# Two small DMAs ahead of ScalarE's first work: one word of every eighth row of x[0] and of w_in

## The chip, the cores and the metric

The kernel runs on one core of a Trainium2 chip. The metric is the device time of one execution in microseconds (us); the median over several executions is compared. A core has five engines that run beside each other, each with its own queue of instructions: PE (TensorE, the matmuls; PEld is its weight load), DVE (VectorE), ACT (ScalarE), POOL (GpSimd) and SP (SyncE, which here only issues DMAs). ScalarE, GpSimd and SyncE issue DMAs from their own instruction queues; sixteen DMA engines move the data for all of them.

## The reference, cut to what matters

```
x:     8 x 8 x 512 x 64   (batch, head, token, dim)
state: 8 x 8 x  32 x 64
attention, per batch and head:
  xread = softmax(x @ state.T / 8) @ state      # 512 x 64
  sread = softmax(state @ x.T / 8) @ x          #  32 x 64
  rows  = concat(xread, sread), heads side by side   # 544 rows of 512 per batch
MoE-like layer on the 8 * 544 = 4352 rows:
  h   = rows @ w_in                  # w_in 512 x 2048
  g   = h + sin(alpha * h)**2 / (alpha + 1e-9)
  out = g @ w_out                    # w_out 2048 x 512, out 4352 x 512 fp32
```

All inputs are fp32 in HBM; the matmuls run in bf16.

## The kernel before

The work is cut into named steps, the methods of the class Steps. The string ORDER lists them, with their arguments, in the order in which they are given out; every engine gets its own instructions in that order, and waits between engines are put in from the data. There is nothing else that schedules: moving a step in ORDER moves its instructions on each engine that it uses.

The steps that matter at the start are these.

- Loads. `l_alpha` (line 222) puts alpha's 16 rows of 128 words into SBUF, issued by ScalarE. `l_s01` (L229) loads the states of batches 0 and 1, and `lq` (L241) loads x of batch 0 in four parts of two heads each, both issued by SP in fp32. All other loads are issued by GpSimd and cast to bf16 on the way: `li` (L262) a quarter of w_in's columns, `lx` (L255) x of a later batch, `l_st` (L247) the other states, `lo` (L268) a quarter of w_out.
- `exp_table` and `sin_table` are one-element activations that bring in ScalarE's tables for Exp and Sin (each shows as an ACT_TABLE_LOAD and an ACTIVATE, L217 and L220).
- `warm_up` (L277) issues matmuls on zeros.
- `al_t` transposes alpha on TensorE (L294); `al_c` and `inva` make alpha and 1/alpha on VectorE. `s01_c`, `s01_t`, `s01_k` bring the first states into their transposed form stT.
- `xq` (L330, ScalarE) casts a part of x[0] to bf16, `xtq` transposes it, `xc` (L362) copies it out as xT. `sc`, `ex`, `rs`, `rr`, `nm` are scores, exponential, row sums, reciprocal and the normalised A. `at` and `ac` transpose A of batch 0 on TensorE; for later batches `ad` (L420, SP) does it as a DMA transpose into AT.
- The first matmul of the layer takes two halves: `m` (L468) multiplies state and w_in into M, copied out by `me` (L476), and `h` or `hg` (L493, L508) multiplies M and AT. `si`, `sq`, `gt` make g, and `o` (L543) multiplies g and w_out; `oc` and `os` copy and store the result.

ORDER begins, before the change:

```
l_alpha l_s01 consts lq.0.S zero.0 ident_ exp_table warm_up.6.512.0 zero.1 lq.1.S lq.2.S identf.V
lq.3.S s01_c.G li.0 xq.0.A al_t.1 s01_t.2 lx.1.0.1 al_c xq.1.A inva xtq.0.3 s01_k.1.V s01_k.0.A li.1
```

So ScalarE's queue starts with the issue of alpha's load, the Exp table load and the dummy Exp, and then waits for the first part of x. TensorE starts with six warm-up matmuls, and then has alpha's transpose.

Of the kernel before, what the change touches and what calls it, by code (L numbers as in the profile page):

```python
# [13 lines left out]
FP32 = mybir.dt.float32  # L14
# [4 lines left out]


ORDER = """
l_alpha l_s01 consts lq.0.S zero.0 ident_ exp_table warm_up.6.512.0 zero.1 lq.1.S lq.2.S identf.V
lq.3.S s01_c.G li.0 xq.0.A al_t.1 s01_t.2 lx.1.0.1 al_c xq.1.A inva xtq.0.3 s01_k.1.V s01_k.0.A li.1
xtq.1 xq.2.A xc.0.0.0.V warm_up.2.128.4 warm_up.2.128.5 xc.0.0.1.V l_st xq.3.A xtq.2.6 sc.0.0.7
xc.0.1.0.V lo.0 xtq.3 ex.0.0 xc.0.1.1.V warm_up.2.128.0 warm_up.2.128.1 warm_up.2.128.2
# [126 lines left out]
class Steps:  # L152
# [65 lines left out]

    def sin_table(k):
        k.nc.scalar.activation(k.tiny[:, 1:2], k.warm[:, 0:1], ACT.Sin)  # L220

    def l_alpha(k):
        k.alpha_rows = k.const.tile([k.FT, k.P], FP32, name="alpha_rows")
        k.nc.scalar.dma_start(k.alpha_rows[:], k.alpha.rearrange("(ft p) -> ft p", p=k.P))
# [395 lines left out]
```

## Time and profile before

| | |
|---|---|
| median of 4 runs | 225.77 us (225.35, 225.46, 226.09, 227.63) |
| the profiled execution | 227.63 us, of which the span in the profile is 225.8 us |
| PE busy | 212.5 us, 94% of the span |
| ACT, DVE, POOL busy | 172.3, 167.9, 109.0 us |
| bytes read from HBM and written to it | 17.44 and 8.91 MB |
| granted TensorE clock, mean | 0.992 of full speed |

The profile shows one execution. Its page gives the busy time of each engine, the span in 40 slices of 5.6 us with the busy share of each as a digit (9 is 90% or more), the TensorE clock that was granted in each slice, and the share of the time in which the 16 DMA engines were moving packets. The chain is the work that ended last, followed back from the last instruction to what released it. In a timeline a line gives start, duration, engine, line, operation and operands, and in brackets how long the engine was idle before it and what ended the wait. An engine name with a q (ACTq, SPq) is an instruction that issues a DMA. "To landing" is the time from a DMA's issue to its completion.

### The profile page before, as it was taken

To read this page: it belongs to the slowest core of one execution; us is meant where nothing else is said; L and a number is where in the kernel's file an instruction comes from. 1 tells how busy PE (TensorE), PEld (TensorE's weight loads), DVE (VectorE), ACT (ScalarE), POOL (GpSimd) and SP (SyncE) were. 2 spreads that over 40 slices of the span, in tenths; PEclk is the share of its full clock that TensorE was granted. 3 is DMA by queue.
4 is the path that set the end of the run, shared out by engine and by line. 5 is a ranking of instruction groups with operands and counts; after the bars stand their busy time and mean duration, and the time that the engine had idled before them with its cause. 6 is when DMAs were issued, how large, how long until landed. Compare 5 with 4: busy or idle time off the path is not lost.

```text
span 225.8 us, 4227 instructions
## 1 busy us (share of the span) xinstructions
PE 212.5 (94%) x1575; PEld 102.4 (45%) x1575; DVE 167.9 (74%) x292; ACT 172.3 (76%) x291; POOL 109.0 (48%) x117
## 2 busy tenths in 40 slices
PE   6678994999999999999999999999999999999993
PEld 2444441343544344444443444444446465555641
DVE  4768773599999989887999877798874779875210
ACT  4789894599999999895997698799861599794111
POOL 6759550385817585786372544196022057451000
PEclk9999998899999999999999999999999999999999
DMA  6999993096795221567514536460026111101332
GB/s 208 174 207 206 208 197 39 15 160 202 138 186 105 85 46 52 107 124 160 75 46 84 152 96 104 77 191 4 0 93 94 50 49 46 46 0 49 90 97 93
DMA packets 37828, 23.48 MB, mean 104 GB/s; under 512 B 20768, under 2 KB 33456, under 8 KB 37808
## 3 DMA queue, kind: packets, MB, share of 16 engines
q1 hardware_dynamic: 26128, 15.08, 24.9%
q0 software_dynamic: 11648, 8.13, 24.8%
q8 instruction: 12, 0.20, 0.4%
q14 instruction: 8, 0.07, 0.1%
q10 hardware_dynamic: 32, 0.01, 0.0%
HBM read 17.44 MB, written 8.91 MB: 117 GB/s over the span
## 4 chain that ended last, share of the span: by engine, by line
PE 84%; ACT 5%; DMA 4%; DVE 4%; issue 1%; POOL 0%
PE o_ps L543 50%; PE h_ps L493 22%; DMA AT<-A 4%; PE m_ps L468 3%; PE h_ps L499 3%; PE w_ps L430 2%; ACT s L516 2%; PE warm_ps L277 2%; PE s_ps L378 1%; DVE gT L532 1%; PE w_ps L441 1%; ACT M L476 1%; ACT L220 1%; DVE R L389 1%; POOL A L195 0%
## 5 line engine op out<-in xcount | busy, mean ns | idle before, releaser
L543 PE MATMUL o_ps<-w_out_sb,gT 128*128 128x512 bf16 (+1 forms) x560 | 137.2, 376 | 0.5 <-DVE stT L314 0.5
L195 POOL TENSOR_TENSOR s<-s 128x512 bf16<-128x512 bf16 (+1 forms) x80 | 80.6, 1020 | 70.7 <-ACT s L516 62.7
L532 DVE SCALAR_TENSOR_TENSOR gT<-s,inva_sb,h_ps 128x512 bf16<-128x512 bf16 (+1 forms) x144 | 97.0, 713 | 18.3 <-POOL s L195 11.9
L516 ACT ACTIVATE s<-h_ps,alpha_sb 128x512 bf16<-128x512 f32 (+1 forms) x144 | 88.6, 669 | 11.5 <-PE h_ps L493 8.8
L543 PEld LDWEIGHTS <-gT 128*128 128x128 bf16 x560 | 53.1, 98 | 60.6 <-issue 5.7
L493 PE MATMUL h_ps<-AT,M 128*128 128x512 bf16 x224 | 61.5, 381 | 3.1 <-DMA AT<-A 3.1
L493 PEld LDWEIGHTS <-M 128*128 128x128 bf16 x224 | 21.6, 98 | 28.4 <-DMA AT<-A 3.6
L525 ACT ACTIVATE s<-s 128x512 bf16<-128x512 bf16 (+1 forms) x54 | 32.3, 605 | 0.9
L476 ACT CAST M<-m_ps 128x512 bf16<-128x512 f32 x36 | 19.5, 592 | 9.9 <-PE m_ps L468 9.8
L551 ACT COPY o_sb<-o_ps 128x512 f32<-128x512 f32 (+1 forms) x14 | 7.8, 557 | 22.3 <-PE o_ps L543 22.2
L195 POOL TENSOR_TENSOR A<-E,rR 128x512 bf16<-128x512 bf16 x14 | 14.5, 1049 | 18.9 <-issue 7.2
L476 DVE CAST M<-m_ps 128x512 bf16<-128x512 f32 x28 | 18.4, 677 | 4.3 <-PE m_ps L468 4.1
L551 DVE COPY o_sb<-o_ps 128x512 f32<-128x512 f32 x21 | 14.3, 687 | 9.3 <-PE o_ps L543 9.0
L389 DVE TENSOR_REDUCE R<-E 128x16 f32<-128x512 bf16 x16 | 10.4, 666 | 0.7 <-ACT E L385 0.6
L468 PE MATMUL m_ps<-w_in_sb,stT 64*32 64x512 bf16 x256 | 10.6, 382 | 0.3 <-ACT xT L362 0.2
L508 PE MATMUL h_ps<-AT,M 128*128 128x512 bf16 x32 | 9.1, 381 | 1.7 <-ACT M L476 1.5
L448 DVE RECIPROCAL rC<-w_ps 128x128 f32<-128x128 f32 x8 | 7.5, 942 | 4.2 <-PE w_ps L441 4.2
L385 ACT ACTIVATE E<-s_ps 128x512 bf16<-128x512 f32 x16 | 8.9, 596 | 1.4 <-PE s_ps L378 1.3
L499 PE MATMUL h_ps<-xs_all,w_in_sb 128*128 128x256 bf16 x64 | 8.9, 273 | 0.0
L516 ACT ACT_TABLE_LOAD x6 | 7.7, 1283 | 0.9 <-PE h_ps L493 0.8
L322 DVE COPY xp<-xnat 128x1024 bf16<-128x1024 bf16 x14 | 7.1, 534 | 1.0 <-DMA xnat<-in_x_dram 1.0
L385 ACT ACT_TABLE_LOAD x6 | 7.7, 1283 | 0.1
(57 smaller groups left out, 96.1 us busy)
## 6 DMA issues: line engine op xcount, KB each, us to landing
out_dram<-o_sb SPq DMA_DIRECT2D x33, 256.0 KB, 2.4
xnat<-in_x_dram POOLq DMA_DIRECT2D x7, 512.0 KB, 6.3
w_in_sb<-in_moe_w_in_dram POOLq DMA_DIRECT2D x4, 512.0 KB, 13.1
w_out_sb<-in_moe_w_out_dram POOLq DMA_DIRECT2D x4, 512.0 KB, 18.0
x<-in_x_dram SPq DMA_DIRECT2D x4, 256.0 KB, 3.7
st_nat<-in_state_dram POOLq DMA_DIRECT2D x1, 256.0 KB, 12.2
out_dram<-o_sb SPq DMA_DIRECT2D x2, 128.0 KB, 2.7
s<-in_state_dram SPq DMA_DIRECT2D x1, 128.0 KB, 2.1
```

Of the source, the lines that this page charges most:

```text
L195: {"V": k.nc.vector, "G": k.nc.gpsimd}[eng].tensor_tensor(out, a, b, ALU.mult)
L385: k.nc.scalar.activation(E[:, g], k.t["sc", b, g][:], ACT.Exp, scale=k.scale)
L389: k.nc.vector.reduce_sum(R[:, g], k.t["E", b][:, g].rearrange("p c (h j) -> p (c h) j", j=k.Ns), axis=AX.X)
L468: k.nc.tensor.matmul(k.t["m", b, s + n, g][o0:o0 + k.Ns, :], k.stT[k.half(r), b * k.G + g, c0:c0 + k.Ns], k.w_in_sb[k.half(r), 2 * g + h, ...
L476: k.copy(eng)(k.t["M", b][:, g, s * k.FW:(s + 1) * k.FW], k.t["m", b, s, g][:])
L493: k.nc.tensor.matmul(hp[:, :n], k.t["M", t][:, g, fs], k.t["AT", t][:, g, :], start=(g == 0), stop=(g == k.G - 1),)
L499: k.nc.tensor.matmul(hp[:, :n], k.w_in_sb[:, q, fs], k.xs_all[:, q].rearrange("p b j -> p (b j)"), start=(q == 0), stop=(q == k.Q - 1),)
L516: k.nc.scalar.activation(s[:, :n], k.t["h", t, f][:, :n], ACT.Sin, scale=k.alpha_sb[:, f:f + 1])
L525: k.nc.scalar.activation(s2[:, :n], s[:, :n], ACT.Square)
L532: k.nc.vector.scalar_tensor_tensor(gT[:, :n], k.t["s2", t, f][:, :n], k.inva_sb[:, f:f + 1], k.t["h", t, f][:, :n], ALU.mult, ALU.add,)
L543: k.nc.tensor.matmul(k.t["o", t, st, half][:, cols], k.t["gT", t, f][:, rows], k.w_out_sb[:, f, cols], start=(f == 0), stop=(f == k.FT - 1),)
L551: k.copy(eng)(o_sb[:, cols], k.t["o", t, st, half][:, cols])
```

## The change

Two new steps, `touch_x` and `touch`, stand first in ORDER, ahead of `l_alpha`. Each issues one DMA from ScalarE's queue into a tile of its own which nothing reads. `touch_x` takes the first word of every eighth 1 KB row of each head of x[0]: 16 rows for each of 8 heads. `touch` takes the first word of every eighth row of w_in: 16 rows in each of the four groups of 128 rows. Every word is a run of 4 bytes by itself.

```diff
 ORDER = """
-l_alpha l_s01 consts lq.0.S zero.0 ident_ exp_table warm_up.6.512.0 zero.1 lq.1.S lq.2.S identf.V
+touch_x touch l_alpha l_s01 consts lq.0.S zero.0 ident_ exp_table warm_up.6.512.0 zero.1 lq.1.S lq.2.S identf.V
...
+    def touch(k):
+        k.touched = k.const.tile([16, k.Q], FP32, name="touched")
+        k.nc.scalar.dma_start(
+            k.touched[:].unsqueeze(2), k.w_in.rearrange("(q p) f -> p q f", p=k.P)[::8, :, 0:1]
+        )
+
+    def touch_x(k):
+        k.touched_x = k.const.tile([16, k.H], FP32, name="touched_x")
+        k.nc.scalar.dma_start(
+            k.touched_x[:].unsqueeze(2),
+            k.x[0].rearrange("h (p i) d -> p h (i d)", i=k.C)[::8, :, 0:1],
+        )
```

## The prediction

> **What bounds the kernel now.** I read first the page's busy rows with the slices, then the chain that ended last in its first 40 us, then the timeline of the start and of the place where TensorE falls idle, then short windows, and last the DMA transfers.
>
> ```profile
> PE   6678994999999999999999999999999999999993
> PEclk9999998899999999999999999999999999999999
> DMA  6999993096795221567514536460026111101332
> PE 84%; ACT 5%; DMA 4%; DVE 4%; issue 1%; POOL 0%
> ```
>
> Each digit is a slice of 5.6 us. TensorE is full from the eighth slice (39.5 us) to the end, and the chain is TensorE for 84% of the span. Only the first six or seven slices have room, and there the DMA engines are full. An edit that touches only the start can move the end only through the moment at which TensorE becomes full. This is the chain around both edges of that stretch:
>
> ```profile
> 1.19 2.74 PE warm_ps L277 x6
> 3.93 0.23 PE al_ps L294
> ...
> 28.29 9.12 DMA AT<-A
> ```
>
> At its front stand the six warm-up matmuls, then the transpose of alpha, which is next in TensorE's order, and through al_c, inva and s01_k it reaches the scores. At its back stands the DMA transpose of batch 1's A, and there TensorE runs dry (timeline, then windows whose columns are the busy time of PE, PEld, DVE, ACT and POOL, PEclk, the DMA share and GB/s):
>
> ```profile
> 37.45 0.60 PE L493 MATMUL h_ps<-AT,M 128*128 128x512 bf16 x2 [3.15 <-DMA AT<-A]
> 34.70:38.20 3.50, 0.75 (x4) 0.40 (x5) 1.35 (x3) 0.54 (x2) 0.00 (x0) 0.99 0.17 19
> 38.20:41.60 3.40, 3.40 (x10) 0.89 (x9) 0.75 (x1) 1.96 (x3) 0.04 (x1) 0.50 0.01 2
> ```
>
> TensorE waits 3.15 us for AT, and the 3.4 us after it run at half the clock. The transpose is not slow by itself: the seven have a median of 3.1 us from issue to landing, this one 9.1. It shares the engines with the queued loads: the DMA share is 1.23 from 28 to 30 us and 1.35 from 30 to 34, and the last load of that backlog, batch 2's xnat, lands 21.1 us after its issue at 16.14, so at 37.2, just before AT at 37.4. **So the start is bound by the bytes of the load stream, and the work in front of TensorE has 3.15 us to spare.**
>
> **The change, part by part.** It removes nothing. It puts two DMA issues ahead of all that ScalarE does, with 16x8 and 16x4 single words, 192 words of 4 bytes, on a queue of its own that so far carried alpha's rows alone. The instruction orders of the other engines are the same in both programs. The eight DMA semaphores go round in turn, so each SP transfer now uses one two places on, and AT's issue gains a wait for touch_x, which is over some 25 us earlier: nothing.
>
> ```profile
> 0.73 0.42 ACTq L224 DMA_DIRECT2D alpha_rows<-in_moe_alpha_dram  x1
> 1.19 1.28 ACT L217 ACT_TABLE_LOAD   x1 [1.19 <-PEq L604]
> 1.20 1.95 SPq L241 DMA_DIRECT2D x<-in_x_dram  x4
> 2.48 0.20 ACT L217 ACTIVATE tiny<-warm 128x1 f32<-128x1 bf16 x1
> 3.94 0.62 ACT L330 CAST xp<-x 128x512 bf16<-128x512 f32 x1 [1.26 <-DMA x<-in_x_dram]
> ```
>
> (1) *ScalarE's issue time.* An issue takes 0.42 us here for alpha and 1.95/4 = 0.49 on SP, so two cost 0.84 to 0.98; I take 0.9. Behind them wait alpha's issue, the Exp table load (1.28) and the dummy Exp (0.20). These end at 2.68 now and at 3.58 then. ScalarE next waits for x until 3.94 (1.26 us idle), so 0.36 of the cover is left and the price is nothing. Without that cover it is 0.9.
>
> (2) *Alpha's landing.* Issued at 0.73, alpha's last completion is in the trace at 2.60, 1.87 later. Issued at 1.63 it lands at 3.50. TensorE wants it at 3.86, after the warm-ups; 0.36 of cover is left, if the words ahead of it do not hold up its queue.
>
> (3) *The words themselves.* 192 words on 16 engines are 12 on each. No transfer of such words is in the trace. The nearest rows are its packet records: a 1024-byte packet of x takes 0.046 us, a 4-byte completion record 0.009, a first 512-byte packet of alpha up to 0.116. So 12 words are 0.11 to 0.55 us per engine, spent between 1.95 (where alpha's first packet stands now) and 2.85 (where it would then stand): alpha is not delayed by them. [...] I take 0.046, so 0.55 us per engine, and keep a twelve times larger value for the slow rival.
>
> (4) *The loads beside them.* From 2.0 to 3.0 us the DMA share is 0.71 and 0.85, so some 0.2 us per engine is free. The other 0.35 falls on state and x: x lands up to 0.35 later (3.92, 4.84, 5.90, 6.60 now). ScalarE's four casts of x sit on or close to the chain there, so the cost to the start is 0 to 0.35.
>
> (5) *What it may give.* First accesses are visibly slow. Of the 1061 packets of state and x before 5.2 us 19 took over 0.1 us, 3.6 us together, 2.7 above the usual. Of the first w_in packets (5.2 to 7 us) seven took 0.42 to 0.87 instead of 0.098, 3.3 us above it. If the touches take all that on themselves, 6.0/16 = 0.38 us per engine comes off the load stream. The touch of x can save little of its part: it is issued at 0.73, the loads of x themselves from 1.20. I take 0.2 for w_in. An earlier w_in helps no compute: m waits only 0.30 us for it, and then for ScalarE, which is in the Sin table load and the AT copy until 11.56. It helps only if AT lands earlier. But the last backlog load ends on thirteen engines by 35.2 and on the last three at 37.0 to 37.2. One of the late engines was late at w_in's first slice (10.64 against 9.30 for the other fifteen); others fell behind at 16 and 28 us, where the records show an instruction fetch of 16 KB. AT waits for all of them, so the saving at the end is 0 to 0.2. I take 0.
>
> **Sum.** A start 0 to 0.35 us later goes into the 3.15 us for which TensorE waits for AT; A is ready that much later, yet AT still lands with the end of the backlog. Change: 0, with -0.2 and +0.35 (if AT follows its issue after all) as ends. The profiled execution took 227.63 us, 225.80 of it span, and is the slowest of the four; the median is 225.77. That spread is larger than any term above. The half clock after the gap, 3.4/2 = 1.7 us, would explain it if not every execution has it. [...] I leave it out of the sum and put it in the range. **Forecast: 225.7 us, no change.** A measurement of this kernel tells about 1%, 2.3 us, from no change.
>
> **The rivals.**
>
> *Faster.* The touches clear the first accesses on the engine that is last, and AT lands up to 1.34 us earlier (10.64 - 9.30). The gap then is below 2 us and the half clock goes for good: 1.34 + 1.7 = 3.0, so 222.7 us. For it: the slow first packets are real, and there is one late engine from w_in's first slice on. Against it: two other engines are as late by 37 us for another reason.
>
> *Slower.* The touches pay the cold price word by word: 12 words at the mean of the seven cold w_in packets (4.0/7 = 0.57) are 6.8 us on each engine. Alpha then lands near 1.95 + 6.8 + 0.65 = 9.4 instead of 2.60, where 0.65 is what it takes now from first packet to last completion. Alpha's transpose starts 5.5 us later, the idle wait gives back 3.15, and 2.4 us remain; the load stream, which shares these engines, would lose as much again where it cannot pass them. I put it at +3.5, so 229.2 us. It decides against me from alpha landing later than 3.86 + 3.15 = 7.0 us. For it: each touched row of w_in may be a first access. Against it: only some ten of the first packets of w_in were cold, not one for each row.
>
> *It does not do what it says.* The touches run beside the first loads instead of ahead of them, and the same cold packets appear as before. Time: 225.8; this is inside no change.
>
> **How the numbers follow.** Forecast together with the idle touch 0.76, faster 0.11, slower 0.13. The middle case has -0.2 to +0.35 from the terms and about one us on either side from the half clock that comes and goes: 224.6 to 226.9. Cut into both rivals until no more than 2 in 10 is left out: 224.0 to 227.8. The chances of over 1% faster, within 1% and over 1% slower are the three above.
>
> **What would show it.** In the profile after: the Exp table load begins near 2.1 us and the first cast of x still near 3.9 to 4.3; al_ps starts between 3.86 and 4.3; AT lands at 37 to 38 us, and TensorE's wait for it is 2.5 to 3.5 us; few w_in packets over 0.4 us. The forecast is wrong if al_ps starts after 7 us, if AT lands before 36 or after 39 us, or if TensorE has a new idle stretch after 45 us.

## The result, and the profile after

The changed kernel takes 225.62 us (median of 35 runs, 224.73 to 228.53), the kernel before, with its runs on the same chips, 226.46 us (56 runs, 225.07 to 228.96). The ratio is 0.9966, with a 95% interval of 0.9947 to 0.9986: a third of one per cent, or 0.77 us, faster. The ratios, and the counts and means of executions below, leave out runs that took over 1.5% longer than the fastest of their kernel. The profiled execution took 224.96 us, 223.2 of it span, against 225.8 before. That is 2.6 us less, three times what the medians differ by, so the pair of profiles must not be read as the effect.

First the slices and the chain's shares of the page after:

```profile
PE   5868999999999999999999999999999999999993
PEclk9999999999999999999999999999999999999999
DMA  6999995494876302759215438440017111101322
PE 84%; ACT 5%; DMA 4%; DVE 3%; issue 1%; POOL 0%; ACTq 0%
```

The dip that TensorE had in its seventh slice is gone, and the clock row has no 8 any more. The chain in the first 40 us, in order of time, shows what stands at both edges now:

```profile
1.67 3.22 DMA alpha_rows<-in_moe_alpha_dram
...
5.02 0.27 PE al_ps L308
...
30.29 6.35 DMA AT<-A
```

At the front stands alpha's load instead of the warm-ups. Alpha's transpose starts at 5.02 instead of 3.86 us, A is ready and AT issued at 30.29 instead of 28.29, and AT lands at 36.6 instead of 37.4. So in this pair of executions the work in front came 2 us later, and the wait behind it ended 0.8 us earlier. The timeline of the changed kernel's start, and then the first matmul on AT:

```profile
0.73 0.42 ACTq L231 DMA_DIRECT2D touched_x<-in_x_dram  x1
1.19 0.45 ACTq L225 DMA_DIRECT2D touched<-in_moe_w_in_dram  x1
1.67 0.47 ACTq L238 DMA_DIRECT2D alpha_rows<-in_moe_alpha_dram  x1
2.17 1.28 ACT L217 ACT_TABLE_LOAD   x1 [2.17 <-issue]
3.46 0.20 ACT L217 ACTIVATE tiny<-warm 128x1 f32<-128x1 bf16 x1
4.56 1.32 ACT L344 CAST xp<-x 128x512 bf16<-128x512 f32 x2 [0.89 <-DMA x<-in_x_dram]
5.02 0.25 PE L308 MATMUL al_ps<-ident_f,alpha_rows 16*128 16x16 f32 x1 [1.09 <-DMA alpha_rows<-in_moe_alpha_dram]
9.03 1.49 PE L291 MATMUL warm_ps<-warm 128*128 128x128 bf16 x12
36.68 0.60 PE L507 MATMUL h_ps<-AT,M 128*128 128x512 bf16 x2 [0.37 <-DMA AT<-A]
```

The last line is the main one: TensorE waits 0.37 us for AT where it waited 3.15. The twelve warm-ups at 9.03 take 1.49 us; in the timeline before they take 0.83:

```profile
7.87 0.83 PE L277 MATMUL warm_ps<-warm 128*128 128x128 bf16 x12
```

So TensorE ran at 0.56 of that speed there, although the clock row shows a 9: the trace's clock record begins at 11.57 us, with full speed, and the view takes what comes before as full. In the profile before it begins at 4.03. The windows behind AT, after (columns as before: PE, PEld, DVE, ACT, POOL, PEclk, DMA share, GB/s):

```profile
34.70:38.20 3.50, 3.13 (x15) 1.23 (x14) 2.81 (x4) 3.22 (x7) 1.43 (x2) 1.00 0.41 48
38.20:41.60 3.40, 3.40 (x23) 1.40 (x22) 2.68 (x5) 2.72 (x5) 1.24 (x2) 1.00 0.01 2
```

TensorE is at work through both and has no half clock: 23 matmul records in the second instead of 10.

**Where the 2.6 us are.** The first matmul that needs AT starts at 36.68 instead of 37.45, which is 0.77. From there to the end it is 186.49 instead of 188.35 us: 1.86 of half clock. This table is from the traces of the profiled executions of the runs below (us; "full clock from" is where the clock record begins, the rest is the span less the start of the first matmul on AT, and the last column has the half-clock windows of 3.41 us):

| kernel | al_ps | full clock from | AT issued | AT lands | TensorE's wait | first matmul on AT | span | rest | half clock from |
|---|---|---|---|---|---|---|---|---|---|
| before | 3.86 | 4.03 | 28.29 | 37.41 | 3.15 | 37.45 | 225.80 | 188.35 | 38.16 |
| changed | 5.02 | 11.57 | 30.29 | 36.63 | 0.37 | 36.68 | 223.17 | 186.49 | |
| changed, again | 4.92 | 12.46 | 30.36 | 36.98 | 0.65 | 37.03 | 223.52 | 186.49 | |
| words of state | 4.78 | 8.56 | 29.05 | 37.45 | 2.43 | 37.50 | 224.00 | 186.50 | |
| words of state, again | 4.79 | 9.29 | 30.36 | 36.96 | 0.63 | 37.00 | 223.54 | 186.54 | 12.71 |
| touches behind alpha | 3.86 | 9.89 | 30.64 | 37.43 | 0.82 | 37.47 | 224.00 | 186.52 | 13.31 |
| nine warm-ups | 5.14 | 6.44 | 30.16 | 37.99 | 1.87 | 38.04 | 224.72 | 186.68 | 13.27 |
| alpha late, no touches | 5.07 | 13.63 | 31.51 | 37.70 | 0.21 | 37.74 | 224.37 | 186.63 | |
| batch 2's load beside AT | 3.86 | 4.50 | 29.70 | 37.75 | 2.08 | 37.80 | 226.03 | 188.23 | 11.32, 38.63 |
| the same with touches | 4.84 | 10.57 | 31.17 | 38.17 | 1.03 | 38.22 | 224.72 | 186.50 | 13.98 |

The rest is 186.5 to 186.7 us in all but two, and these two are the ones with a half-clock window right behind the wait. With a half-clock window at 12.7 to 14 us alone the rest is 186.50 to 186.68 us, without any it is 186.49 to 186.63. AT is issued over a range of 3.2 us and lands within 1.5. So, in these executions, an edit at the start is worth what it does to the landing of AT, and to the 1.7 to 1.9 us that a half clock behind it costs.

**After which waits the clock halved.** The half-clock windows of the table begin at whole multiples of 3.413 us from where the clock record of their execution begins, to within 0.01: 38.16 is 34.13 us behind 4.03, ten times 3.413, 38.63 as far behind 4.50; 13.27 is two behind 6.44, and 13.31 one behind 9.89. So the waits are counted here in steps of 3.413 us from the first clock record of each execution; these steps fall differently in each. The work left is rough, as the ends of matmuls are modelled. The wait of 3.15 us lay inside one step, from 34.75 to 38.16, which had 0.71 us of TensorE's work, and a half clock followed. The wait of 2.08 us lay inside one step as well, from 35.22 to 38.63, which was left with 1.33 us of work, and a half clock followed. The wait of 2.43 us was cut by an edge at 35.87 us, which left 2.60 and 1.78 us on its two sides, and none followed. The other waits of the table left 2.4 us or more in each step, and none followed. In the changed kernel the step from 11.57 to 14.98 us had 1.70 us of work, and none followed that either. So in these executions what a wait cost went with where it fell among the steps as well as with its length.

**How much of the 2 us is the change.** Not all of it need be. The kernel with work in the wait (below) starts exactly as the kernel before, yet its AT was issued at 30.11 us, 1.8 later. Its eight transposes of the first states, below those of the kernel before:

```profile
4.08 0.41 PE L283 MATMUL st_ps<-ident,s01b 128*64 128x128 bf16 x8
4.08 0.64 PE L283 MATMUL st_ps<-ident,s01b 128*64 128x128 bf16 x8
```

They go with a clock that was full only from 12.54 us, against 4.03; the last two parts of x also landed 0.75 us later there. One and the same start thus differs by nearly 2 us between two executions, and the pair of profiles cannot tell this from the 1.16 us by which alpha's transpose came later. The two executions of the table with a long rest are also the two with a full clock before 5 us; AT was issued early in them, at 28.29 and 29.70, and the wait was long. Whether the two issues make such executions rarer was not tested by itself.

### The profile page after: what moved, and what is told of

Read it like the earlier page. It is cut to its first block, busy times and chain, and to the rows that moved or that the text cites. A ratio compares the mean times of both kernels' runs of the same rounds, so it can differ in the third digit from the quotient of the medians.

```text
span 223.2 us, 4230 instructions
## 1 busy us (share of the span) xinstructions
PE 212.9 (95%) x1575; PEld 104.2 (47%) x1575; DVE 167.8 (75%) x292; ACT 172.2 (77%) x291; POOL 108.9 (49%) x117
## 4 chain that ended last, share of the span: by engine, by line
PE 84%; ACT 5%; DMA 4%; DVE 3%; issue 1%; POOL 0%; ACTq 0%
PE o_ps L557 50%; PE h_ps L507 22%; PE m_ps L482 3%; PE h_ps L513 3%; DMA AT<-A 3%; PE w_ps L444 2%; ACT s L530 2%; PE s_ps L392 1%; DMA alpha_rows<-in_moe_alpha_dram 1%; DVE gT L546 1%; PE w_ps L455 1%; ACT M L490 1%; ACT L220 1%; PE warm_ps L291 1%; PE x_ps L351 1%
## 5 line engine op out<-in xcount | busy, mean ns | idle before, releaser
L513 PEld LDWEIGHTS <-w_in_sb 128*128 128x128 bf16 x64 | 6.3, 98 | 3.2 <-DVE xs_all L465 0.2
```

The costliest lines, as they stand in the source:

```text
L513: k.nc.tensor.matmul(hp[:, :n], k.w_in_sb[:, q, fs], k.xs_all[:, q].rearrange("p b j -> p (b j)"), start=(q == 0), stop=(q == k.Q - 1),)
```

## The experiments

Two theories of the gain were set against each other. Delay: the two issues make alpha late, TensorE starts later, idles less before AT and meets the half clock less often. Warmth: the words take the slow first accesses off the loads, and the load stream ends earlier.

**Words of other data, twice.** The touches take the same number of words from the states of batches 0 and 1, which are loaded at that moment anyway.

```diff
-    k.touched[:].unsqueeze(2), k.w_in.rearrange("(q p) f -> p q f", p=k.P)[::8, :, 0:1]
+    k.touched[:].unsqueeze(2), k.state[0:2].rearrange("b h j d -> (b h) j d")[:, 8:12, 0:1]
...
-    k.x[0].rearrange("h (p i) d -> p h (i d)", i=k.C)[::8, :, 0:1],
+    k.state[0:2].rearrange("b h j d -> (b h) j d")[:, 0:8, 0:1],
```

> The two DMAs stay first on ScalarE's queue with the same number of single words, but take them from the states of batches 0 and 1, which the kernel loads at the same moment, so that no page of x or w_in is touched ahead. Delay theory (alpha comes late behind the two issues, TensorE starts 1 to 2 us later, idles less before AT and loses less to the half clock): alpha's transpose starts near 5.0 us again and the time is that of the changed kernel, ratio to before 0.995 to 0.998. Warmth theory (the words take the slow first accesses off the loads): the gain is gone, ratio 1.000 to 1.004, and seven or so w_in packets over 0.4 us come back. If what made alpha late was slow first accesses to w_in ahead of it, alpha lands near 3.5 instead of 4.9.

> The words from the states instead of x and w_in once more, since the first look had fourteen executions. Delay theory: ratio to before 0.996 to 0.999 and granted clock 1.0 in about half of the executions, as in the changed kernel. Warmth theory: 1.000 or more.

Ratios 1.0009 (0.9982 to 1.0036) and 0.9981 (0.9949 to 1.0013): neither is clear of 1, so the time decides between the theories neither way. The chain and the timeline of the first:

```profile
1.67 2.98 DMA alpha_rows<-in_moe_alpha_dram
4.78 0.27 PE al_ps L308
...
37.50 0.61 PE L507 MATMUL h_ps<-AT,M 128*128 128x512 bf16 x2 [2.43 <-DMA AT<-A]
```

Alpha is as late with words that touch nothing new (2.98 us after its issue, against 3.22), so slow first accesses ahead of it are not what holds it up. The trace has the words themselves at 0.009 us each. What remains is the company it is issued in: its issue comes at 1.67, beside the second part of x, and from 3 to 5 us the DMA share is 0.95 or more in the profiles before and after; and two DMAs of words stand ahead of it in its own queue. Which of the two holds it up was not separated. With alpha first it needed 1.9 us.

**The changed kernel again.**

> The changed kernel itself again, on the same chip as the alpha delay without touches, since the effect is a third of one per cent. Both theories: ratio to before 0.995 to 0.999, granted clock 1.0 in about half of the executions. Delay theory: the same ratio and the same share as with alpha late and no touches. Warmth theory: lower than that by 0.003.

Ratio 0.9987 (0.9961 to 1.0013), not clear of 1 by itself. With the first measurement the mean span over 52 executions is 223.93 us (standard error 0.11); with the words of state it is 224.12 over 34 (0.16), and before 224.33 over 151 (0.07). Taken together, over several chips, the changed kernel is 0.40 us faster than before; between the two sources of words the difference of 0.19 is one standard error.

The share of executions with a mean granted clock of at least 0.997 is 26 of 52 and 15 of 34, against 8 of 151 before. This looks like the cause, and it is not. Of the executions of the kernel before with a span under 225 us, the 7 with such a clock have a mean span of 223.97 us and the other 110 one of 223.95; with the change it is 223.70 (26) and 223.77 (21). The table shows why. In the kernel before one half-clock window, behind the wait, puts the mean at 0.992; in four more rows the mean is 0.992 as well, with the window at 12.7 to 14 us, ahead of the wait. This is the clock row of the touches behind alpha, with the half clock in its third slice and a rest of 186.52 us:

```profile
PEclk9969999999999999999999999999999999999999
```

The span says more. The two executions of the table with the half clock behind AT have 225.8 us and more, the others 224.7 and less. Executions of 225 us or more are 34 of 151 before, 5 of 52 with the change and 6 of 34 with the words of state. Roughly half of the 0.40 us is this share; the rest is that the shorter executions are shorter, 223.73 instead of 223.95 us. A cut at 225 was chosen after the result, and the counts are small, so this is an indication only.

**The touches behind alpha.**

```diff
-touch_x touch l_alpha l_s01 consts
+l_alpha touch_x touch l_s01 consts
```

> Both touches as in the change, but after alpha's issue instead of ahead of it, so alpha is not delayed. Delay theory: alpha's transpose starts at 3.9 us, the wait for AT is about 3 us, ratio to before 0.999 to 1.001. Warmth theory: the w_in words still run some 2 us ahead of the first w_in packet, so the gain stays, ratio 0.995 to 0.998, with last w_in completion before 10.3 us and AT landing before 36.8.

Ratio 0.9993 (0.9961 to 1.0025); full clock in 0 of 19 executions, and 225 us or more in 5. Alpha's transpose is back at 3.86 us and the gain is not seen, which would speak for delay; but the interval does not exclude 0.997. In its profile 14 w_in packets before 7 us took over 0.3 us, more than the 8 of the kernel before, though all words had landed at 4.94 and the first w_in packets come after 5 us. In the two profiles of the changed kernel there are 2 and 3, with the words of state 4, with alpha late 4 and with nine warm-ups 5. These packets do not follow the touches.

**Nine warm-ups, without and with the touches.**

```diff
-exp_table warm_up.6.512.0
+exp_table warm_up.9.512.0
```

> The kernel before, without touches, with nine warm-up matmuls instead of six: 3 x 0.43 to 0.46 = 1.3 us more in front of alpha's transpose. Delay theory: start 1.3 us later, wait for AT 1.8 instead of 3.1 us, no half clock after it, so ratio to before 0.993 to 0.998. Warmth theory: no gain from a delay, ratio 1.000 to 1.006.

> The changed kernel with nine warm-up matmuls instead of six, so that TensorE is busy until alpha lands and the idle second between them is gone; alpha's transpose starts near 5.2 instead of 5.0 us. If it is the idle stretch, through the state of the clock, that separates the changed kernel: granted clock 1.0 in few executions (nine warm-ups without touches: 4 of 22), ratio to before 0.999 to 1.003. If it is the later start alone, or warmth: clock does not matter, ratio 0.995 to 0.999.

Ratios 1.0007 (0.9978 to 1.0035) and 0.9985 (0.9955 to 1.0015); full clock in 4 of 18 and 10 of 18, and 225 us or more in 6 of 18 and 4 of 18. Delaying alpha's transpose by 1.3 us of busy TensorE brings no gain, so a later start alone is not enough: the wait fell to 1.87 us, as delay expects, but AT landed at 37.99. With the touches the share of full clock is high although the idle second is filled, but that share does not carry the time, and the counts of long executions are too small to tell the theories apart.

**Alpha late without touches.** Alpha's load is issued by SP behind the second part of x.

```diff
-zero.1 lq.1.S lq.2.S
+zero.1 lq.1.S l_alpha lq.2.S
...
-        k.nc.scalar.dma_start(k.alpha_rows[:], k.alpha.rearrange("(ft p) -> ft p", p=k.P))
+        k.nc.sync.dma_start(k.alpha_rows[:], k.alpha.rearrange("(ft p) -> ft p", p=k.P))
```

> No touches. Alpha's load is issued by SP after the second part of x instead of by ScalarE, so that it lands near 4.9 us as in the changed kernel, and TensorE stands idle for about 1 us between the warm-ups and alpha's transpose. Delay theory (the gain of the change comes from alpha's lateness alone, through the state of the TensorE clock): granted clock 1.0 in about half of the executions (before: 5 of 67, changed: 18 of 36), ratio to before 0.995 to 0.998. Warmth theory: ratio 1.000 to 1.006, clock 1.0 as rarely as before.

Ratio 1.0030 (1.0008 to 1.0053), slower; full clock in 10 of 22. The mean clock is as delay expects; the time is not. In the profile

```profile
37.74 0.61 PE L493 MATMUL h_ps<-AT,M 128*128 128x512 bf16 x2 [0.21 <-DMA AT<-A]
```

the wait is used up: the last part of x landed at 9.14 us, AT was issued at 31.51, and TensorE's other work reached to 37.5. The last part of x landed at 6.60 in the kernel before, so this edit delays more than alpha. It reaches the far end of the cover, and that makes the run no clean test of the gain.

**Work in the wait.** Twelve matmuls on zeros in front of the first matmul on AT.

```diff
-gt.0.13 h.1.6.4
+gt.0.13 warm_up.12.512.4 h.1.6.4
```

> The kernel before, without touches, with twelve matmuls on zeros (12 x 0.216 = 2.6 us) put in front of the first matmul that needs AT, so that TensorE is busy in its wait. If the half clock after this wait costs 1.7 us in the executions that have it: granted clock 1.0 behind the wait, ratio to before 0.993 to 0.998, with alpha, start and load stream as before. If the half clock is not what separates the two kernels: ratio 0.999 to 1.003.

Ratio 1.0048 (1.0025 to 1.0071), slower. From the timeline:

```profile
35.96 2.75 PE L277 MATMUL warm_ps<-warm 128*128 128x512 bf16 x12
```

The expectation took the wait for a fixed one. In this execution TensorE was ready at 36, AT landed at 37.05, and the filler ended at 38.7. It kept the clock full behind the wait and cost 1.7 us, as much as the half clock costs.

**Batch 2's load moved: beside AT, without and with the touches.**

```diff
-sc.1.0.4 lx.2.0.1 gt.0.1
+sc.1.0.4 gt.0.1
...
-ad.1 si.0.8
+ad.1 lx.2.0.1 si.0.8
```

> No touches. The load of batch 2's x, the last of the backlog that AT shares the engines with, is issued after AT instead of ahead of it. If the end of the load stream sets AT, and AT sets the end: AT lands 2 to 4 us earlier (33 to 35 us), TensorE's wait for it falls from 3.1 to under 1 us, and no half clock follows: ratio to before 0.985 to 0.992. If AT is slow by itself: AT still lands at 37 us, ratio 0.999 to 1.003.

> The changed kernel with the same move of batch 2's load behind AT. Delay theory: with the wait for AT gone, a later start is no longer absorbed, so the touches give nothing or cost up to 1 us beside the same move without them: ratio to before 0.986 to 0.997, not below the move alone. Warmth theory: the touches bring their 0.3% again, ratio lower than the move alone by 0.003.

Ratios 1.0024 (0.9999 to 1.0049) and 1.0003 (0.9978 to 1.0029). GpSimd issued the load at 29.61, SP issued AT at 29.70: both ran together and AT landed at 37.75. The half clock follows in the windows of the first:

```profile
34.00:37.80 3.80, 1.72 (x9) 0.59 (x7) 2.81 (x4) 2.54 (x5) 1.54 (x2) 1.00 1.23 130
38.60:42.00 3.40, 3.40 (x17) 1.04 (x14) 0.75 (x1) 1.90 (x3) 0.21 (x1) 0.50 0.01 2
```

The gain that was expected did not come: the load had not been taken out of AT's time, only to its front edge.

**The same load moved behind the wait, without and with the touches.**

```diff
-sc.1.0.4 lx.2.0.1 gt.0.1
+sc.1.0.4 gt.0.1
...
-sq.0.14.G gt.0.10
+sq.0.14.G lx.2.0.1 gt.0.10
```

> No touches. The load of batch 2's x stands behind the last square that GpSimd has before the wait, so that it is issued near 34 us, when AT's packets have moved, and not at the same moment as AT as in the first move of it. If the sharing of the engines with the loads is what makes AT late: AT lands between 33 and 35 us, TensorE's wait for it is below 0.5 us, no half clock behind it, ratio to before 0.984 to 0.992. If not: AT at 37 us again, ratio 0.999 to 1.004; batch 2's cast would wait if its load, due near 41 us, lands after 43.

> The same place for batch 2's load, with the touches. Delay theory: nothing absorbs the later start any more, so it costs what A is ready later, 0.5 to 2 us: ratio to before 0.988 to 1.000, and 0.002 to 0.009 above the same move without touches. Warmth theory: 0.003 below it.

Ratios 1.0242 (1.0193 to 1.0290) and 1.0245 (1.0175 to 1.0315): slower, with the touches and without them alike. AT does what was expected. The time to landing of the seven transposes in the first, its longest being this AT:

```profile
DMA to landing us min/median/max: 3.0/3.1/4.9
```

It landed at 34.8 (33.5 with the touches) instead of 37.4, and TensorE did not wait for it. AT took 4.9 us from issue to landing here and 9.1 in the kernel before, so the loads beside it are what makes it late. The chain and the waits show where the gain went:

```profile
35.69 5.90 DMA xnat<-in_x_dram
41.59 0.02 issue
41.61 1.61 DVE xp L322 x2
...
43.31 8.23 DMA xT<-xp
```

```profile
PE s_ps L378 <- DMA xT<-xp: 3.8, 1, 3.8
DVE xp L322 <- DMA xnat<-in_x_dram: 2.1, 1, 2.1
```

Batch 2's x lands at 41.6; VectorE waits for it with everything queued behind the cast; its transpose is issued at 43.31, just after batch 3's load at 42.88, shares the engines with that and takes 8.23 us, where it took 4.3 in the kernel before; and TensorE waits 3.8 us for it. The collision has only moved on by one batch. A version that moves batch 3's load as well was not tried, so no kernel here gains from the earlier AT.

## Why the prediction was right or wrong

**The end is set by AT and the load stream, with cover for the start: right.** A was ready 2.0 us later in the profiled pair and nothing of it reached the end. Moving the load out of the way brought AT to 34.8, and leaving it there held AT at 36.6 to 38.2 for issues from 28.3 to 31.5.

**(1) ScalarE's issue time: right.** Two issues moved the table load from 1.19 to 2.17, 0.98 us. The first cast of x came at 4.56, waiting for x and not for the table.

**(2) Alpha's landing: wrong.** It was to land at 3.50 and landed at 4.89. The step took the 1.87 us of an issue at 0.73 for an issue at 1.67; behind two DMAs of words and beside the parts of x it is 3.22, and 2.98 with words of state. The cover of 0.36 us was gone, and TensorE waited 1.09 us.

**(3) The words: the size was off the other way.** They took 0.009 us each and not 0.046, so 0.11 us per engine. The slow rival, at 0.57 each, did not occur.

**(4) x: partly.** Its parts landed 0.62, 0.40, 0.09 and 0.06 us later than before, where up to 0.35 was taken. Together with (2) and with slow matmuls up to 11.57 us (twelve warm-ups in 1.49 instead of 0.83), the start was 2.0 us late and not 0 to 0.35. But an unchanged start was 1.8 us late in another execution, with the clock and x alone; the clock at the start was in no term.

**(5) First accesses: taken as worth nothing at the end, and nothing was shown.** The count of slow w_in packets does not go with the touches. A gain of up to 0.2 us from it stays inside the intervals.

**The sum.** It had 0, with the half clock left out, and it is right as to the range: the change stayed far below 1%. That 225.62 us stands so near to 225.7 is luck: the forecast added nothing to 225.77 us of four runs, and 56 runs of the kernel before have 226.46. The measured change, 0.77 us faster at the first measurement and 0.4 of mean span with the second, is inside the forecast's range but beyond its own terms' end of 0.2. In the pair of profiles the term that was left out, the half clock, is 1.86 of 2.6 us, together with an AT that landed 0.8 earlier. The faster rival named both pieces, but not their cause: AT was not earlier through cleared first accesses as far as these runs show.

**The half clock, left out of the sum: wrong.** No run shows a ground for leaving it out. In the profile before, the wait of 3.15 us left 0.71 us of work in its step of 3.413, and the half clock followed. A wait 0.35 us shorter would have left an estimated 1.06 (0.71 + 0.35), still less than the 1.33 behind which it followed in the run with batch 2's load beside AT. The waits below 2 us in the table, 0.21 to 1.87, left 2.4 us or more of work in each step, and none followed.

**The signs.** The table load came at 2.17 us and one w_in packet took over 0.4 us, as forecast (with the words of state, one and none). The first cast (4.56), al_ps (5.02), AT's landing (36.63) and the wait (0.37) all missed their ranges. None of the three that would have made the forecast wrong came about.

**What stays open.** The changed kernel is faster by 0.1 to 0.3%, and in its two profiles the wait for AT is short and no half clock follows. What in the change brings this about is not shown. Alpha's lateness is a candidate, through the clock at the start or through the wait, but alpha late without touches was slower for its own reason, and the words of state are clear neither of the kernel before nor of the changed one. Whether any of it needs words of x and w_in is not settled either.

## What to carry to other kernels

Before costing an edit at the start, find the wait at which the start's work rejoins the rest; a delay in front is free up to the length of that wait, and in the pair of profiles here even 2 us were. What bounds such a wait may be a transfer's share of the engines, which neither an earlier nor a somewhat later issue changed here (AT landed at 36.6 to 38.2 us for issues from 28.3 to 31.5); taking a load out of its way only helps if the load's own consumer still has time (it brought AT to 34.8, and a wait of 3.8 us for batch 2). When the expected effect is a fraction of a per cent, compare many executions: one pair of profiles differed here by 2.6 us, the kernels by less than 0.8. And a mean clock says nothing of the time until it is known where the half clock stood: ahead of a wait it cost nothing here, behind it 1.7 to 1.9 us.

## What the runs showed of the hardware that was not expected

A DMA of 16 rows that took 1.9 us from issue to landing took 3.0 to 3.2 when issued 0.9 us later, beside 512 KB of queued x and behind 192 words in its own queue. Single-word packets took 0.009 us each, a fifth of a 1 KB packet's 0.046. A half-clock window came after waits of 3.15 and 2.08 us and did not come after one of 2.43: of the steps of 3.413 us in which these waits lay, the first two had 0.71 and 1.33 us of TensorE's work, those of the third 2.60 and 1.78. And the clock row shows full speed until the first record: in the changed kernel twelve matmuls took 1.49 instead of 0.83 us under a 9.
